# Spatial weights loaded and converted inside the last attention steps of batch 0

## The chip, the cores and the metric

The kernel runs on one core of a Trainium2 chip. The metric is the device time of one execution in microseconds (us). The kernel before took 498.06 us (median of three runs, 496.54 to 500.2).

## The reference

Three blocks follow each other, for a batch of 4 with 576 tokens and 512 channels:

```python
# 1 attention, 8 heads of 64, four with a local and four with a strided mask
scores = where(mask, q @ k.T / 8, -1e9);  x = softmax(scores) @ v
# 2 gated block: h, then a mix over tokens with the spatial weights
h = relu(x @ w_in);  u, v = halves of h
v_n = (v - mean(v)) / sqrt(var(v) + 1e-6)
v_s = einsum('ts,bsd->btd', w_spatial, v_n) + b_spatial
x = (u * v_s) @ w_out
# 3 angles, a mix over tokens, and a residual product
theta = x @ w_theta;  zr, zi = x * cos(theta), x * sin(theta)
y = x + w_tok_r mixed zr + w_tok_i mixed zi;  out = y + relu(y @ w_ch)
```

The weights of w_in, w_out, w_theta, w_tok and w_ch arrive as float64 and are turned into pairs of float16 (high and low part) on the chip. The spatial weights arrive as float32. A matrix product of such pairs is three float16 products (high by high, low by high, high by low).

## The kernel before

Four batches pass one after another. For each, `main_v` makes v (TensorE), relu and mean and variance (ScalarE and VectorE), and `norm`, which normalises v and splits it into `vn`. `main_mid` makes four column blocks of u (`u_chunk`), of the token mix (`sp_chunk`, which reads `vn` and the spatial weights `wsp`, `wspt`), then x2 and theta; `main_end` makes the token mix y and the last product.

Attention of batch 0 has nothing to hide behind. `attention0` runs it in eleven steps (s = 0 to 10) over eight groups of blocks, as a pipeline: in step s TensorE makes the scores of group s (into `pm`), VectorE shifts them, ScalarE takes the exponential; group s-1 is transposed into the bank `av` and copied by ScalarE; group s-2 is multiplied by its values; group s-3 goes into `xT`. `av` is one single bank: whatever writes it in step s waits until ScalarE has copied the group of step s-1 out of it. In steps 1 to 5 a step begins with `WARM` = 6 products of an identity matrix into `av`, whose result nobody reads.

Other work is put into the steps by the dictionary handed to `attention0`: three lists per step, run before, in the middle and at the end of it. It holds the conversions of w_in. Each of eight blocks (`wv[0..3]` for v, `wu[0..3]` for u; `win_piece`) has a load on SP's queue ([0]), two ScalarE instructions ([1], [2]), one VectorE instruction ([3]), and the split into the high part (ScalarE) and the low part (GpSimd) ([4]). `go` advances `main_v(0)` by one part, `step` starts batch 1's attention, which loads its first k, q and v.

While the names in `pinned` are set, that is until `pinned.clear()` after `attention0`, each engine and SP's queue run what is issued in the order of the program. What comes later is ordered by a planner, and may pass the pinned work where an engine would otherwise stand. The later conversions (`conv`) are called by `others()` at due times, counted in TensorE's columns.

The spatial weights: `CONV_SP` gives three due times, which `others()` meets only after `attention0`. `sp_part(0)`, `sp_part(2)` and `sp_tail` each load a block into a staging region, make the high part on ScalarE and the low part on VectorE. The regions are raw0 (`x2f`) and raw1 (the front of `zf`), in which `wv[0]`, `wv[1]` and `wv[2]`, `wv[3]` are staged before. The mask of batch 3 is loaded by `load_mask16`; its tile shares three buffers with those of u.

Of the kernel before, what the change touches and what calls it, by code (L numbers as in the profile page):

```python
# [14 lines left out]
F32 = mybir.dt.float32  # L15
# [3 lines left out]
AF = mybir.ActivationFunctionType  # L19
ALU = mybir.AluOpType  # L20
# [4 lines left out]
SPS = 1024.0  # L25
# [30 lines left out]
WARM = 6  # L56
LEAD = 3.0
ATT_AT = (None, (2.7, 4.2), (86.0, 5.4), (174.5, 4.6))
PREP_AT = (112.0, 126.0, 131.0)
CONV_SP = (20.0, 9.9, 1.9)  # L60
CONV_OUT = (37.0, 12.0, 5.0)
CONV_TH = (49.0, 17.0, 5.0)
TOK_AT = (27.5, 29.5)
# [7 lines left out]
def kernel(  # L71
# [52 lines left out]
    nc = Engines  # L124
# [17 lines left out]
    B, DM, S = out.shape  # L142
    P = 128
    NC = DM // P
    NF = S // P
    T0 = NF * P
    TL = S - T0
# [47 lines left out]
    wsp = const.tile([P, 2, NF, S], F16, name="wsp")  # L195
    wspt = const.tile([P, 2, S], F16, name="wspt")
# [21 lines left out]
    def s2(name):  # L218
        return scr.tile([P, 2, HS * 2], F32, tag="s2", name=name, bufs=4)
# [4 lines left out]
    def pm(name):  # L224
        return ps_m.tile([P, 2, 512], F32, tag="pm", name=name)

    def pa(tag):
        return ps_a.tile([P, 512], F32, tag=tag, name=tag)
# [11 lines left out]
    early = [True, 0]  # L240


    raw0 = x2f.rearrange("p c n -> p (c n)").bitcast(I64)
    raw1 = zf[:, 0:8 * S].bitcast(I64)
# [4 lines left out]
    def stage(late_raw=None):  # L249
        i = early[1]  # L250
        early[1] += 1
        if early[0]:
            return (raw0, raw1)[i % 2], vals[i % 2]
        return late_raw, s2("wx").rearrange("p a n -> p (a n)")
# [21 lines left out]
    def pair(ap, n):  # L276
        return ap[:, 0:2 * n].rearrange("p (a n) -> p a n", a=2)
# [27 lines left out]
        for i in range(0, NC, 2):  # L305
            yield lambda i=i: prep_w(dst, src, slice(0, DM), i, late)

    def sp_part(i):
        stg = pair(stage()[0].bitcast(F32), S)
        nc.sync.dma_start(stg, w_spT[i * P:(i + 2) * P, :].rearrange("(a p) n -> p a n", p=P))  # L310
        nc.scalar.activation(wsp[:, 0, i:i + 2, :], stg, AF.Copy, scale=SPS)
        nc.vector.scalar_tensor_tensor(wsp[:, 1, i:i + 2, :], stg, SPS, wsp[:, 0, i:i + 2, :],
                                       op0=ALU.mult, op1=ALU.subtract)

    def sp_tail():
        stg = pair(stage()[0].bitcast(F32), S)
        for j in range(2):
            nc.sync.dma_start(stg[j * TL:(j + 1) * TL, 0, :], w_spT[T0:S, :])
        nc.scalar.activation(wspt[:, 0, :], stg[:, 0, :], AF.Copy, scale=SPS)
        nc.vector.scalar_tensor_tensor(wspt[0:TL, 1, :], stg[0:TL, 0, :], SPS, wspt[0:TL, 0, :],  # L320
                                       op0=ALU.mult, op1=ALU.subtract)

    def bias_load():
        t = s1("bias")
        for r in (TL, 96):
            nc.gpsimd.dma_start(t[r:r + 1, :], b_sp)
        return t

    def bias_hi(t):
        for r in (TL, 96):  # L330
            nc.scalar.activation(wspt[r:r + 1, 1, :], t[r:r + 1, :], AF.Copy, scale=SPS)
# [130 lines left out]
    def load_q(b, hp, q, c0, c1, by):  # L462
        by.dma_start(q[:, c0:c1], qp[b, hp][:, c0:c1])

    def load_k(b, hp, k, c0, c1, by):

        local = hp < 2
        src = kzl[b, hp] if local else kzs[b, hp - 2]
        c0, c1 = (c0 + STRIDE if c0 else 0, c1 + STRIDE) if local else (c0, c1)
        for j in range(2):  # L470
            h = slice(64 * j, 64 * j + 64)
            by.dma_start(k[h, c0:c1], src[h, j, c0:c1])

    def load_qk(b, hp, q, k, c0, c1, by=None):
        load_q(b, hp, q, c0, c1, by or nc.sync)
        load_k(b, hp, k, c0, c1, by or nc.sync)
# [173 lines left out]
    def attention0(aside):  # L650

        xf = xT[1].rearrange("p e c n -> p (e c n)").bitcast(F32)
        vf = wtok.rearrange("p e i n -> p (e i n)").bitcast(F32)
        qk = kts + [xf[:, i * 2 * S:(i + 1) * 2 * S].rearrange("p (j n) -> p j n", j=2) for i in range(2)]
        q, k = [t[:, 0] for t in qk], [t[:, 1] for t in qk]
        v01 = vf[:, 0:18 * VW].rearrange("p (h n d) -> p h n d", h=2, n=9)
        v23 = vf[:, 18 * VW:30 * VW].rearrange("p (h n d) -> p h n d", h=2, n=6)
        v = [v01[:, i] for i in range(2)] + [v23[:, i] for i in range(2)]  # L660
        for hp in (2, 3):
            load_q(0, hp, q[hp], 0, S, nc.sync)
            load_k(0, hp, k[hp], 0, S, nc.scalar)
        nc.scalar.activation(x2f[:, 0, 0:1], halfpi, AF.Exp)
        bias = bias_load()
        make_masks()
        for n in range(2):
            nc.gpsimd.memset(v23[:, n, 0:6, 0:VW:VW - 1], 1.0)
            nc.gpsimd.memset(v01[:, n, 0:9, 0:VW:VW - 1], 1.0)
        load_vs(0, v23, (2, 3), range(5, 8), nc.gpsimd)  # L670
        load_vs(0, v23, (2, 3), range(5))
        for hp in range(2):
            load_qk(0, hp, q[hp], k[hp], 0, S)
        load_vs(0, v23, (2, 3), range(8, 11))
        load_vl(0, v01, (0, 1))
        for f in aside[-1]:
            f()
        bias_hi(bias)
        un = {}
        for s in range(NG + 3):  # L680
            pre, mid, end = aside.get(s, ((), (), ()))
            if 1 <= s < 6:
                wt = pa("av")
                for _ in range(WARM):
                    nc.tensor.matmul(wt[:, 0:P], identb, identb, start=True, stop=True)
            if s < NG:
                sc = pm("a0")
                t = s2("smx")
                sm, pT = t[:, 0, 0:512], t[:, 1, 0:512].rearrange("p (n k) -> p n k", n=4)
                st = att_p.tile([P, 2, 8], F32, tag="st", name="st", bufs=4)  # L690
                un[s] = sm, pT, st
                qd_scores(quads0[s], q, k, sc)
                qd_shift(quads0[s], sc, sm, st)
            for f in pre:
                f()
            if s >= 3:
                sm, pT, st = un.pop(s - 3)
                local = quads0[s - 3][0]
                qd_out(0, quads0[s - 3], pT, pm("xt")[:, 0, :] if local or s == 5 else pa("sc"))
            if 1 <= s <= NG:  # L700
                sm, pT, st = un[s - 1]
                qd_turn(quads0[s - 1], sm, pa4("av"), pT)
            if s < NG:
                qd_exp(quads0[s], un[s][0])
            if s == 0:
                bias_lo(bias)
            for f in mid:
                f()
            if 2 <= s < NG + 2:
                sm, pT, st = un[s - 2]  # L710
                local = quads0[s - 2][0]
                qd_pv(quads0[s - 2], v, pT, pa("sc").unsqueeze(1) if local else pm("pv"), st, pT)
            for f in end:
                f()
# [277 lines left out]
    def main_v(b):  # L992
# [52 lines left out]
        if b == 0:  # L1045
            ps = []

            def some(pr, cs, ts=(0, 1)):
                for c in cs:
                    for t in ts:  # L1050
                        v_mm(ps[pr][:, t, :], 2 * pr + t, c)

            ps.append(pm("v0"))
            some(0, V0_ORDER[:1])
            yield
            some(0, V0_ORDER[1:2])
            ps.append(pm("v1"))
            some(1, V0_ORDER[:2])
            yield
            some(0, V0_ORDER[2:3])  # L1060
            some(1, V0_ORDER[2:3])
            yield
            for pr in range(2):
                some(pr, V0_ORDER[3:])
                v_relu(pr, ps[pr])
            yield
            norm((0, 1))
        for pr in V_ORDER if b else V_ORDER[2:]:
            ps = pm(f"v{pr}")
# [176 lines left out]
    def timed(parts, due, lead, gap):  # L1246
        parts = list(parts)
        for i, f in enumerate(parts):
            conv.append((due - lead - gap * (len(parts) - 1 - i), f))

    timed([lambda i=i: sp_part(i) for i in range(0, NF, 2)] + [sp_tail], *CONV_SP)
    timed(sq_parts(wout, w_out), *CONV_OUT)
    timed(sq_parts(wth, w_th), *CONV_TH)
    conv.append((conv[-1][0], switch))
# [10 lines left out]
    for at, f in [(at, lambda n=n: tok_load(*toks[n])) for n, at in enumerate(TOK_AT)] + [  # L1265
            (at, lambda: next(atts[N32])) for at in PREP_AT] + [(15.0, load_mask16)]:
        i = next((i for i, c in enumerate(conv) if c[0] > at), len(conv))
# [30 lines left out]
        nc.tensor.matmul(wt[:, 0:P], ident, ident, start=True, stop=True)  # L1298
    wv, wu = ([win_piece(half, i, by) for i in range(NC)] for half, by in ((1, nc.sync), (0, nc.sync)))
    v0 = main_v(0)  # L1300

    def go():
        next(v0)
# [3 lines left out]
        4: ((), (), [w[0] for w in wu]),  # L1307
        5: ((), (), wv[2][1:3]),
        6: ((), wv[2][3:4], wv[2][4:] + wv[3][1:3]),
        7: ((), wv[3][3:4], wv[3][4:] + wv[0][1:3] + [go, step]),  # L1310
        8: ((), wv[0][3:4], wv[0][4:] + wv[1][1:3] + [go]),
        9: (wv[1][3:], (), wu[0][1:3] + [go]),
        10: (wu[0][3:] + wu[1][1:4], (), wu[1][4:] + wu[2][1:3] + [go]),
    })
    for f in wu[2][3:] + wu[3][1:]:
        f()
    pinned.clear()
    run_main(v0)
# [93 lines left out]
```

## Time and profile before

| | |
|---|---|
| time, median of three runs | 498.06 us |
| profiled execution | 498.24 us, its span 496.5 us |
| TensorE (PE) busy | 471.1 us, 95% of the span |
| VectorE (DVE) busy | 306.8 us, 62% |
| ScalarE (ACT) busy | 269.5 us, 54% |
| GpSimd (POOL) busy | 75.8 us, 15% |
| mean granted TensorE clock | 0.990 |

A busy share is a mean over stages that have different limits. The stage of interest is the first 85 us. An instruction in the timeline has a start, a duration, the idle time of its engine before it, and what ended this idle time. Durations of neighbours on ScalarE and VectorE overlap by some tenths of a microsecond, so the distance from start to start is what one costs its engine.

### The profile page before, as it was taken

How to read it: one execution, taken by the hardware profiler on the slowest of the kernel's cores; microseconds unless marked ns; L12 is line 12 of the kernel's file. 1: busy time of each engine (PE TensorE's matmuls, PEld its weight loads, DVE VectorE, ACT ScalarE, POOL GpSimd, SP SyncE). 2: the span in 40 equal slices, each digit the busy share in tenths (PEclk: the TensorE clock that was granted, in tenths of full speed). 3: DMA queues.
4: the chain of work that ended last, by engine and by line, in shares of the span. 5: the costliest groups of instructions: out<-in, count | busy, mean ns of one | idle time of the engine just before them, and what ended most of it. 6: DMA issues, size and time to landing. Idle time of an engine off the chain costs nothing. (4 is left out here: it accounts for less than half of the span.)

```text
span 496.5 us, 10872 instructions
## 1 busy us (share of the span) xinstructions
PE 471.1 (95%) x4476; PEld 353.1 (71%) x4476; DVE 306.8 (62%) x653; ACT 269.5 (54%) x488; POOL 75.8 (15%) x72
## 2 busy tenths in 40 slices
PE   7989687989999999999999999999999999999997
PEld 5754465867577777777658777777657777777775
DVE  4764998877798654863588587872587121217412
ACT  3378677869964344445864766754862022148302
POOL 4014135300004300111002310021005200210220
PEclk9979899999999999999999999999999999999999
DMA  8795647466690045210284156321160020003502
GB/s 205 198 320 177 213 154 239 140 223 176 162 205 1 3 162 164 63 34 1 46 177 127 32 129 175 71 46 20 40 152 2 1 96 1 0 2 68 125 1 96
DMA packets 71421, 52.72 MB, mean 106 GB/s; under 512 B 50713, under 2 KB 59285, under 8 KB 71371
## 3 DMA queue, kind: packets, MB, share of 16 engines
q1 hardware_dynamic: 70843, 51.26, 37.2%
q8 instruction: 35, 0.57, 0.5%
q10 hardware_dynamic: 320, 0.59, 0.5%
q0 software_dynamic: 208, 0.17, 0.1%
q14 instruction: 15, 0.12, 0.1%
HBM read 35.36 MB, written 4.72 MB: 81 GB/s over the span
## 5 line engine op out<-in xcount | busy, mean ns | idle before, releaser
L108 PE MATMUL y<-wtok,zf 128*128 128x288 f16 x864 | 107.2, 286 | 0.0
L108 PEld LDWEIGHTS <-zf 128*128 128x128 f16 x864 | 84.1, 98 | 22.2 <-issue 1.2
L108 PE MATMUL u<-xT,win 128*128 128x288 f16 x384 | 50.9, 291 | 4.6 <-ACT win L108 2.9
L108 PE MATMUL sp<-wsp,vn 128*128 128x288 f16 x384 | 50.2, 286 | 1.3 <-ACT u L108 1.3
L108 PE MATMUL v<-win,xT 128*128 128x512 f16 (+1 forms) x240 | 49.5, 386 | 0.0
L108 PE MATMUL x<-zf,wout 128*128 128x288 f16 x384 | 49.4, 286 | 0.0
L108 PEld LDWEIGHTS <-win 128*128 128x128 f16 x384 | 37.9, 99 | 15.2 <-ACT win L108 3.2
L108 PEld LDWEIGHTS <-vn 128*128 128x128 f16 x416 | 40.5, 98 | 11.3 <-issue 1.4
L108 PE MATMUL th<-x2h,wth 128*128 128x288 f16 x384 | 47.9, 286 | 0.2 <-DVE x2h L108 0.2
L108 PE MATMUL c<-x2h,wch 128*128 128x288 f16 x360 | 45.2, 286 | 0.0
L108 PEld LDWEIGHTS <-wth 128*128 128x128 f16 x384 | 37.6, 98 | 9.8 <-issue 0.4
L108 PEld LDWEIGHTS <-wch 128*128 128x128 f16 x384 | 37.4, 98 | 9.2
L108 PEld LDWEIGHTS <-wout 128*128 128x128 f16 x384 | 36.8, 98 | 9.5
L108 POOL TENSOR_TENSOR x2h<-x2f,x2h 128x576 f16<-128x576 f32 x19 | 27.1, 1429 | 102.8 <-DVE x2h L108 45.1
L108 PEld LDWEIGHTS <-xT 128*128 128x128 f16 (+1 forms) x240 | 21.1, 101 | 25.5 <-issue 2.4
L108 ACT ACTIVATE x2h<-x2f 128x576 f16<-128x576 f32 (+2 forms) x28 | 19.9, 712 | 28.4 <-DVE x2f L108 28.1
L108 ACT ACTIVATE o<-c 128x576 f32<-128x576 f32 x15 | 9.7, 646 | 34.9 <-PE c L108 34.7
L108 DVE TENSOR_TENSOR ta<-ta,x2f 128x1152 f32<-128x1152 f32 (+1 forms) x17 | 21.7, 1283 | 10.9 <-ACT ta L108 10.9
L108 DVE SCALAR_TENSOR_TENSOR x2f<-y,x2f 128x576 f32<-128x576 f32 x16 | 12.0, 753 | 25.1 <-PE y L108 25.1
L108 POOL TENSOR_TENSOR zf<-u,zf 128x576 f16<-128x576 f32 x8 | 10.2, 1281 | 112.6 <-ACT zf L108 112.6
L108 DVE TENSOR_TENSOR u<-u,sp 128x576 f32<-128x576 f32 x16 | 12.0, 750 | 24.1 <-PE sp L108 24.1
L108 DVE SCALAR_TENSOR_TENSOR o<-x2f,o 128x576 f32<-128x576 f32 (+1 forms) x17 | 12.2, 722 | 23.6 <-ACT o L108 23.6
(147 smaller groups left out, 738.4 us busy)
## 6 DMA issues: line engine op xcount, KB each, us to landing
out_dram<-o SPq DMA_DIRECT2D x15, 288.0 KB
kt<-in_qp_dram SPq DMA_DIRECT2D x10, 288.0 KB
qs<-in_qd_dram SPq DMA_DIRECT2D x8, 288.0 KB
zf<-in_w_in_dram SPq DMA_DIRECT2D x4, 512.0 KB
xT<-in_w_ch_dram SPq DMA_DIRECT2D x2, 1024.0 KB
kt<-in_kzl_dram SPq DMA_DIRECT2D x12, 152.0 KB
ks<-in_kl_dram SPq DMA_DIRECT2D x4, 304.0 KB
v<-in_vl_dram SPq DMA_DIRECT2D x8, 144.0 KB
```

What stands on the lines that cost most here:

```text
L108: ins = f(*args, **kwargs)
```

## The change

Without the due times `CONV_SP`, the spatial blocks are handed to `attention0` as steps: the load of the first block in the middle of step 7, its ScalarE half in the middle of step 8, its VectorE half at the end of step 8, with the load of the 64 last rows (the tail) behind it; the load of the second block in step 9 as soon as `wv[1][3]` has read its region; tail and second block are converted in step 10. The conversions of the u blocks each move forward by about half a step, so that `wu[2]` is finished in the middle of step 10 and the ScalarE instructions of `wu[3]` stand between the two last parts of v. `main_v(0)` has one more stop (one `go` for each pair of token blocks of the last channel block), and `early[1] = 1` keeps the alternation of the staging regions. Steps 6 and 7 get `2 * WARM` = 12 idle products each.

```diff
-CONV_SP = (20.0, 9.9, 1.9)
...
-    def sp_part(i):
-        stg = pair(stage()[0].bitcast(F32), S)
...
+    def sp_piece(i, raw):
+        stg = pair(raw.bitcast(F32), S)
+        return [
+            lambda: nc.sync.dma_start(stg, w_spT[i * P:(i + 2) * P, :].rearrange("(a p) n -> p a n", p=P)),
+            lambda: nc.scalar.activation(wsp[:, 0, i:i + 2, :], stg, AF.Copy, scale=SPS),
+            lambda: nc.vector.scalar_tensor_tensor(wsp[:, 1, i:i + 2, :], stg, SPS, wsp[:, 0, i:i + 2, :],
+                                                   op0=ALU.mult, op1=ALU.subtract)]
+
+    def sp_tail(raw):
...
-            if 1 <= s < 6:
+            if 1 <= s < 8:
                 wt = pa("av")
-                for _ in range(WARM):
+                for _ in range(WARM if s < 6 else 2 * WARM):
                     nc.tensor.matmul(wt[:, 0:P], identb, identb, start=True, stop=True)
...
             for pr in range(2):
                 some(pr, V0_ORDER[3:])
                 v_relu(pr, ps[pr])
-            yield
+                yield
             norm((0, 1))
...
-    timed([lambda i=i: sp_part(i) for i in range(0, NF, 2)] + [sp_tail], *CONV_SP)
...
+    sps = [sp_piece(i, raw) for i, raw in ((0, raw1), (2, raw0))] + [sp_tail(raw1)]
+    early[1] = 1
...
-        7: ((), wv[3][3:4], wv[3][4:] + wv[0][1:3] + [go, step]),
-        8: ((), wv[0][3:4], wv[0][4:] + wv[1][1:3] + [go]),
-        9: (wv[1][3:], (), wu[0][1:3] + [go]),
-        10: (wu[0][3:] + wu[1][1:4], (), wu[1][4:] + wu[2][1:3] + [go]),
+        7: ((), wv[3][3:4] + sps[0][:1], wv[3][4:] + wv[0][1:3] + [go, step]),
+        8: ((), wv[0][3:4] + sps[0][1:2], wv[0][4:] + wv[1][1:3] + sps[0][2:] + sps[2][:1] + [go]),
+        9: (wv[1][3:4] + sps[1][:1] + wv[1][4:] + wu[0][1:3], wu[0][3:4], wu[1][1:3] + wu[0][4:] + [go]),
+        10: (wu[1][3:] + wu[2][1:3] + sps[2][1:2], sps[2][2:] + wu[2][3:], sps[1][1:] + [go] + wu[3][1:3] + [go]),
     })
-    for f in wu[2][3:] + wu[3][1:]:
+    for f in wu[3][3:]:
         f()
```

## Rows read from the trace of the kernel before

**Rows 1.** Busy time by stage: us, PE, PEld, DVE, ACT, POOL, granted clock, DMA share, GB/s.

```profile
0.00:25.00 25.00, 21.11 (x337) 16.59 (x341) 15.16 (x40) 9.00 (x17) 6.16 (x21) 1.00 0.78 202
...
29.00:36.00 7.00, 6.31 (x36) 3.89 (x38) 3.10 (x10) 4.88 (x11) 2.33 (x2) 0.51 1.03 354
...
53.00:57.00 4.00, 0.42 (x2) 0.11 (x2) 4.00 (x13) 1.90 (x4) 1.16 (x1) 0.94 0.66 217
57.00:60.00 3.00, 2.98 (x13) 1.92 (x14) 3.00 (x13) 1.90 (x3) 1.02 (x1) 0.51 0.99 365
60.00:69.50 9.50, 8.17 (x98) 6.18 (x97) 9.50 (x25) 8.24 (x12) 3.67 (x4) 1.00 0.43 129
...
110.00:496.50 386.50, 378.99 (x3385) 287.87 (x3382) 223.30 (x457) 197.21 (x365) 44.50 (x31) 1.00 0.30 76
```

**Rows 2.** Timeline, ScalarE, steps 5 to 10 and after: start, us, instruction, idle before.

```profile
25.37 0.58 ACT L108 ACTIVATE smx<-av 96x512 f32<-96x512 f32 x1
...
35.41 0.38 ACT L108 ACTIVATE xT<-xt 128x256 f16<-128x256 f32 x1 [1.70 <-PE xt L108]
...
47.57 2.54 ACT L108 ACTIVATE vr<-v 128x1024 f32<-128x1024 f32 x3
...
50.02 1.15 ACT L108 ACTIVATE wsp<-zf 128x1152 f16<-128x1152 f32 x1
51.07 0.67 ACT L108 ACTIVATE wspt<-x2f 128x576 f16<-128x576 f32 x1
```

**Rows 3.** Timeline, VectorE, from step 6 to the last spatial block.

```profile
26.39 0.55 DVE L108 TENSOR_REDUCE st<-a 128x4 f32<-128x384 f32 x1
...
31.23 0.68 DVE L108 SCALAR_TENSOR_TENSOR x2h<-zf,x2h 128x512 int32<-128x512 int32 x1
...
46.05 1.36 DVE L108 SCALAR_TENSOR_TENSOR wsp<-x2f,wsp 128x1152 f16<-128x1152 f32 x1 [0.32 <-ACT wsp L108]
48.61 0.69 DVE L108 BATCH_NORM_STATS2 bs<-vr 128x6 f32<-128x512 f32 x1 [1.21 <-ACT vr L108]
...
51.74 1.33 DVE L108 SCALAR_TENSOR_TENSOR wsp<-zf,wsp 128x1152 f16<-128x1152 f32 x1
...
53.66 0.73 DVE L108 SCALAR_TENSOR_TENSOR wspt<-x2f,wspt 64x576 f16<-64x576 f32 x1
```

**Rows 4.** Timeline, TensorE, u and the first token mix of batch 0.

```profile
55.78 0.42 PE L108 MATMUL u<-xT,win 128*128 128x288 f16 x2 [2.89 <-ACT win L108]
57.02 4.52 PE L108 MATMUL u<-xT,win 128*128 128x288 f16 x24 [0.82 <-POOL win L108]
...
69.48 1.63 PE L108 MATMUL sp<-wsp,vn 128*128 128x288 f16 x12 [1.33 <-ACT u L108]
```

**Rows 5.** Timeline, TensorE, steps 5 to 8.

```profile
21.95 0.49 PE L108 MATMUL av<-identb 128*128 128x128 bf16 x6
...
24.74 0.56 PE L108 MATMUL a<-kt 64*64 64x96 f32 x16
...
32.20 2.74 PE L108 MATMUL v<-win,xT 128*128 128x512 f16 x6
...
36.47 4.06 PE L108 MATMUL v<-win,xT 128*128 128x512 f16 x18
```

**Rows 6.** Timeline, SP's issues of loads, and one user of a load.

```profile
28.45 0.33 SPq L108 DMA_DIRECT2D kt<-in_qp_dram  x1
...
66.50 0.53 SPq L108 DMA_DIRECT2D zf<-in_w_th_dram  x1
...
73.88 1.17 ACT L108 ACTIVATE zf<-zf 128x1024 f32<-128x1024 f32 x1 [1.01 <-DMA zf<-in_w_th_dram]
```

**Rows 7.** Timeline, GpSimd, low parts of `wu[1]` and `wu[2]`.

```profile
46.61 1.81 POOL L108 TENSOR_TENSOR win<-x2h,win 128x512 f16<-128x512 f32 x1 [1.68 <-ACT win L108]
...
55.80 1.16 POOL L108 TENSOR_TENSOR win<-x2h,win 128x512 f16<-128x512 f32 x1 [7.38 <-ACT win L108]
```

**Rows 8.** VectorE by groups, 44 to 57 us: least, median, most ns; first and last start.

```profile
L108 DVE TENSOR_SCALAR rs<-rs x2: 143/470/796, 55.7 to 56.2; 128x4 int32<-128x4 int32 x2
```

More of the change, by code (lines that the diff above doesn't have):

```diff
@@ L306, in sq_parts, with load @@
             yield lambda i=i: prep_w(dst, src, slice(0, DM), i, late)
-    def sp_part(i):
-        stg = pair(stage()[0].bitcast(F32), S)
[L310 to L321, printed above, removed]
+    def sp_piece(i, raw):
[6 more added lines that the diff above has]
+    def sp_tail(raw):
+        stg = pair(raw.bitcast(F32), S)
+        def load():
+            for j in range(2):
+                nc.sync.dma_start(stg[j * TL:(j + 1) * TL, 0, :], w_spT[T0:S, :])
+        return [
+            load,
+            lambda: nc.scalar.activation(wspt[:, 0, :], stg[:, 0, :], AF.Copy, scale=SPS),
+            lambda: nc.vector.scalar_tensor_tensor(wspt[0:TL, 1, :], stg[0:TL, 0, :], SPS, wspt[0:TL, 0, :],
+                                                   op0=ALU.mult, op1=ALU.subtract)]
     def bias_load():
```

## The prediction

> **What bounds now.** I read the busy time by stage first, then the timeline of each engine from 20 to 85 us. From 110 us on TensorE is busy 379.0 of 386.5 us at clock 1.00 [rows 1]: what the head gains or loses should stay to the end. The head is where the change works, and there TensorE is held up twice: its clock is at 0.51, the lower of its two levels (1.2 GHz of 2.4), from 29 to 36 us and from 57 to 60 us, and from 53 to 57 us it is busy 0.42 of 4 us. The reader should see beside it that VectorE is busy 4.00 of 4, 3.00 of 3 and 9.50 of 9.5 us in the stages from 53 to 69.5 us [rows 1]. From the first statistics of v at 48.61 us, ahead of which it stood 1.21 us for ScalarE's relu of 47.57 us [rows 2, 3], VectorE works off a backlog, at whose end stands the normalised `vn`, and the first token mix, which reads it, starts at 69.48 us [rows 4]. So the question is when VectorE starts on the statistics and how much it has to do from there, not when TensorE has u.
>
> **Idle products.** Six take 0.49 us [rows 5], so twelve take some 0.9. They write `av`, so they also wait for ScalarE's copy out of it, and the scores of the step stand behind them. In step 6 the scores began at 24.74; the copy ended at 25.37 + 0.58 = 25.95 [rows 2, 5]. Now they begin at 25.95 + 0.9 = 26.85, 2.1 us later. VectorE had other work until 26.39 [rows 3] and can shift these scores when they end, near 27.75: 1.4 us later. In step 7, by the same walk, ScalarE and VectorE are 0.7 to 1.2 us late. What they give back: the clock was 1.00 through the steps that have six [rows 1]; if it stays there, six value products cost 1.3 us for 2.74 (eighteen take 4.06, 0.225 each, at the upper level) [rows 5], and the transposes around them some 1.0 us less. TensorE then begins the eighteen products at 35.0 instead of 36.47 us, and ScalarE's first instruction of step 8 starts at 34.7 instead of 35.41 us, before which it stood 1.70 us for TensorE [rows 2, 5]. Term: -0.7 us at the head of step 8, between +0.5 (clock not held) and -1.3.
>
> **First spatial block.** Its load waits for the conversion `wv[3][3]`, which ended at 31.23 + 0.68 = 31.91 us [rows 3] and with the above ends at about 33.0. Batch 1's first loads, issued from 28.45 us [rows 6], stand behind it on SP and slip some 5 us; they are used only after the value products, so I cost that at nothing, and if the cover went, batch 1's first scores would wait. ScalarE reaches the block's high part at about 35.2 us, and if the block isn't there it stands, with `wv[0]`, `wv[1]` and all later conversions behind it. Landing: at least 0.59 MB at the 354 GB/s of that stretch [rows 1], 1.7 us, which costs nothing; at most the 7.4 us of the 1 MB block that was issued at 66.50 behind two other loads and waited for until 73.88 [rows 6]. With nothing ahead of it this block is nearer to the first: I take 3.4 us, landed at 36.4, and ScalarE stands 1.2 us. The Trainium skill ("DMA: Bandwidth & Descriptors", Anatomy of one DMA, stated for loads from GpSimd's queue) gives about 2.0 us plus the bytes at 436 GB/s, an estimate of 3.4 us here; no wait in the trace of before shows this block's landing.
>
> **ScalarE until the relu.** Ahead of the first relu now also stand the second block's high part (50.02 to 51.07, 1.05 from start to start), the tail's (some 0.57) [rows 2] and the high part of `wu[2]` (some 0.5): +2.1 us; the first block's was there before. The two instructions of `wu[3]` (1.1) come before the second relu only. In the pinned order of steps 8 to 10 ScalarE also waits for VectorE, for 0.6 us conversions and the tail's 0.73 us; it did so before, with less VectorE work in between, so I add 0.8. Sum: -0.7 + 1.2 + 2.1 + 0.8 = +3.4; some of it falls where ScalarE stood in before, so I take +2.8: relu at about 50.4, statistics from 51.4 instead of 48.61 us.
>
> **VectorE from there.** It no longer has to do, after that moment, the second block's low part (1.33), the tail's (0.73) and the conversion of `wu[2]` (0.68 by its like), 2.5 us from start to start [rows 3]. Nor does it meet GpSimd's low part of `wu[2]` (55.80 to 56.96 us [rows 7]), beside which a small instruction of the variance took 796 instead of 143 ns [rows 8]: -0.65. Statistics 2.8 later, work 3.2 less: `vn` comes 0.4 us earlier. Against it, the same kind of meeting is new in steps 8 and 9, where the low part of `wsp` (1.36) and GpSimd's low part of `wv[0]` fall together. The row at 46.61 shows such a pair: GpSimd took 1.81 for 1.16 us beside the `wsp` of 46.05 [rows 3, 7]. Between nothing and 1.2 us on VectorE's next conversion I take 0.5. Sum for `vn`: +0.1 us, bounds -1.9 (block landed in time, no meeting) to +3.
>
> The Trainium skill ("SBUF — State Buffer", SBUF: two separate sides) has a rule that speaks against the change here: of a GpSimd instruction and a VectorE one with two inputs in SBUF, the later stands until the other is done. By that rule the conversion of `wv[1]` would stand for all of GpSimd's 1.16 us, and the sum would be 0.7 us longer; rows 8 agree with it for one small instruction, and no row shows it for a conversion.
>
> **TensorE's waits.** The 2.89 and 0.82 us in which u waits for its weights can go, and some 1.5 us of clock (24 products in 4.52 us [rows 4]; by columns, at the rate of the eighteen, 3.0). But the token mix doesn't wait for u: what TensorE saves before 69.48 us it will spend waiting for `vn`, or for the buffers that the later relu sets free, so I count nothing. One thing can move: at 69.48 us it had waited 1.33 us for the relu of the third u block [rows 4], held up by the mask of batch 3, whose load follows TensorE's progress. I take half, -0.65, of 0 to -1.3.
>
> **Sum.** The profiled execution is 498.24 us, span 496.5 and 1.7 around it, 0.2 above the median. 498.24 + 0.1 - 0.65 = 497.7; against the median 497.5. I forecast no change.
>
> **Rivals.** *TensorE is what counts.* If VectorE only looks full, its planner having filled time with work that could wait, and `vn` follows u, the 2.89, 0.82, 1.5 and 1.33 us of TensorE's waits are all won: 498.1 - 6.5 = 491.6 us. For it: TensorE is idle or slow there. Against: VectorE has no idle time from 53 to 69.5 us [rows 1]. Chance 0.12.
>
> *ScalarE stands for the first spatial block.* This wait takes the place of the one removed, in step 8, with the whole pinned order behind it. Each microsecond after 36.4 moves the relu, the statistics and `vn` by one; landing 7.4 us after its issue, like the block of 66.50, gives +4.0: 501.5 us. It decides from 37.5 us on, and is over 1% slower from 41.5. For it: the load is some 2 us old when ScalarE comes to it, and the DMA share is 1.03 in that stretch [rows 1]. Against: w_in's blocks should be through by then, and batch 1's loads queue behind. Chance 0.13.
>
> *The clock falls nevertheless*, and the idle products only hold up the scores: +0.5 instead of -0.7 in step 8, 498.7 us. For it: TensorE mostly waits in steps 6 to 8. Chance 0.07.
>
> **Numbers.** The forecast has 0.68. Its own range is 495.5 to 500, since the bounds -1.9 and +3 hardly come together with those of the other term. To leave no more than 2 in 10 outside I leave out the first rival and the upper half of the second: 494.5 to 501. Within 1% (about 5 us, what can be told from no change here) lie the forecast, the third rival and most of the second: 0.82. Faster by over 1%: 0.11, nearly all the first rival; slower: 0.07, the worst of the second.
>
> **What will show it.** Clock 1.00 from 29 to 36 us, and the eighteen products at about 35 us. A wait of ScalarE for the spatial block in step 8. The first relu of v between 49.5 and 51.5 us, and the statistics right behind it. u without a wait for its weights, but a wait of TensorE for `vn`, buffers or VectorE in its place, and the first token mix at 68.5 to 70 us. I am wrong if the first token mix comes before 66 us, or if the relu is not later than in before.

## The result and the profile after: 0.75% slower

The changed kernel takes 501.91 us (median of 20 runs), the kernel before 498.7 (20 runs beside them): ratio 1.0075 [1.0051, 1.0099], by which it is some 3.75 us slower (the medians lie 3.2 us apart). I had forecast no change (497.5) in a range that ended at 501. The profiled spans are 500.6 and 496.5 us.

The busy time by stage of the changed kernel, columns as in [rows 1]:

```profile
29.00:36.00 7.00, 6.45 (x70) 3.74 (x68) 4.72 (x16) 5.05 (x11) 2.32 (x2) 1.00 0.91 337
53.00:57.00 4.00, 3.66 (x29) 2.54 (x30) 4.00 (x11) 3.25 (x6) 0.00 (x0) 0.50 0.65 255
57.00:60.00 3.00, 3.00 (x19) 2.09 (x18) 3.00 (x14) 2.36 (x3) 1.38 (x1) 0.71 0.00 0
60.00:69.50 9.50, 8.23 (x94) 6.15 (x91) 8.58 (x25) 5.85 (x9) 3.60 (x3) 1.00 0.66 218
66.00:72.00 6.00, 2.23 (x28) 1.42 (x25) 6.00 (x7) 2.98 (x4) 5.87 (x5) 1.00 1.01 345
72.00:79.00 7.00, 6.56 (x41) 4.43 (x42) 6.78 (x13) 5.40 (x9) 1.24 (x2) 0.53 0.01 2
110.00:500.60 390.60, 383.46 (x3435) 291.22 (x3434) 225.85 (x466) 200.37 (x375) 43.43 (x31) 1.00 0.30 77
```

The clock is 1.00 from 29 to 36 us, where [rows 1] had 0.51. From 53 us TensorE has work at once, but at the lower level. The new hole is from 66 to 72 us: TensorE busy 2.23 of 6 us while VectorE is full, and right behind it the clock is 0.53 for seven microseconds. From 110 us on nothing is new: 7.1 us of idle time, 7.5 in [rows 1].

ScalarE, VectorE, GpSimd, TensorE and SP in the same kernel, from their timelines (start, us, instruction, idle before):

```profile
24.73 0.58 ACT L107 ACTIVATE smx<-av 96x512 f32<-96x512 f32 x1
...
36.12 1.16 ACT L107 ACTIVATE wsp<-zf 128x1152 f16<-128x1152 f32 x1 [1.61 <-DMA zf<-in_w_spT_dram]
...
50.25 1.00 ACT L107 ACTIVATE vr<-v 128x1024 f32<-128x1024 f32 x1
```

```profile
38.97 1.27 DVE L107 SCALAR_TENSOR_TENSOR x2h<-x2f,x2h 128x512 int32<-128x512 int32 x1 [0.30 <-ACT x2h L107]
...
51.66 0.68 DVE L107 BATCH_NORM_STATS2 bs<-vr 128x6 f32<-128x512 f32 x1
...
61.00 1.21 DVE L107 SCALAR_TENSOR_TENSOR x2h<-x2f,x2h 128x1024 int32<-128x1024 int32 x1
...
63.15 1.23 DVE L107 SCALAR_TENSOR_TENSOR x2h<-zf,x2h 128x1024 int32<-128x1024 int32 x1 [0.80 <-ACT x2h L107]
...
66.14 5.26 DVE L107 TENSOR_SCALAR vr<-vr,mv,rs 128x512 f32<-128x512 f32 x4
...
72.48 2.34 DVE L107 TENSOR_TENSOR vn<-vr,vn 128x1024 f16<-128x1024 f32 x2
```

```profile
37.88 1.81 POOL L107 TENSOR_TENSOR win<-x2h,win 128x512 f16<-128x512 f32 x1 [3.79 <-ACT win L107]
...
65.90 5.22 POOL L107 TENSOR_TENSOR wout<-x2h,wout 128x512 f16<-128x512 f32 x4 [6.10 <-ACT wout L107]
```

```profile
31.29 1.47 PE L107 MATMUL v<-win,xT 128*128 128x512 f16 x6
34.25 4.06 PE L107 MATMUL v<-win,xT 128*128 128x512 f16 x18
...
54.49 6.54 PE L107 MATMUL u<-xT,win 128*128 128x288 f16 x35
...
72.37 1.12 PE L107 MATMUL sc<-pT,v 96*64 96x64 f32 x16 [4.04 <-DVE rs L107]
...
74.50 5.40 PE L107 MATMUL sp<-wsp,vn 128*128 128x288 f16 x24
```

```profile
32.26 0.39 SPq L107 DMA_DIRECT2D zf<-in_w_spT_dram  x1
...
48.09 0.39 SPq L107 DMA_DIRECT2D zf<-in_w_out_dram  x1
51.76 0.38 SPq L107 DMA_DIRECT2D x2f<-in_w_out_dram  x1
```

Against them five rows of the kernel before that the prediction had not asked for, on VectorE, GpSimd and SP:

```profile
61.91 1.23 DVE L108 SCALAR_TENSOR_TENSOR x2h<-zf,x2h 128x1024 int32<-128x1024 int32 x1
63.05 1.91 DVE L108 TENSOR_SCALAR vr<-vr,mv,rs 128x512 f32<-128x512 f32 x4
...
66.28 3.55 DVE L108 TENSOR_TENSOR vn<-vr,vn 128x1024 f16<-128x1024 f32 x2
```

```profile
64.91 2.28 POOL L108 TENSOR_TENSOR wout<-x2h,wout 128x512 f16<-128x512 f32 x2 [4.77 <-ACT wout L108]
```

```profile
53.10 0.37 SPq L108 DMA_DIRECT2D zf<-in_w_out_dram  x1
```

The reader should see four things. Ahead of the normalise now stand **both** conversions of w_out, with a wait between them (1.21 + 0.80 + 1.23); before, one did. The normalise itself, four `TENSOR_SCALAR`, takes 5.26 us instead of 1.91, beside four low parts of w_out on GpSimd; before, two started when it was nearly over. Part of that price had been paid elsewhere: in the kernel before, GpSimd's work stood beside the low part of `vn`, which took 3.55 us; now that is 2.34 (72.48), 1.2 us less. And the load of w_out's first block is issued 5.0 us sooner than before.

The head of the program runs up to 3 us sooner or later from one profiled execution to the next, so I count from ScalarE's copy of step 5 (25.37 us before, [rows 2]; 24.73 after). Microseconds behind that copy, with the kernels of the next section; "theta" is the first product with w_theta, "v, batch 1" the first of its 60 products in a row, and from there to the end all take 368 to 370 us:

| kernel | relu | normalise | token mix | theta | v, batch 1 | end |
|---|---|---|---|---|---|---|
| before | 22.20 | 37.68 | 44.11 | 89.92 | 102.01 | 471.13 |
| after | 25.52 | 41.41 | 49.77 | 95.13 | 107.37 | 475.87 |
| e1, GpSimd's parts late | 25.93 | 41.98 | 46.55 | 93.76 | 106.02 | 474.67 |
| e2, conversions late | 25.76 | 37.53 | 42.35 | 89.74 | 103.01 | 470.99 |
| e4, before + idle products | 20.67 | 34.95 | 41.21 | 86.82 | 98.58 | 467.09 |
| f2, e4 + u sooner | 21.76 | 35.73 | 41.16 | 86.82 | 98.58 | 466.87 |
| f4, e2 + second block late | 24.50 | 37.14 | 42.65 | 88.75 | 100.51 | 468.57 |
| g1, before + conversions late | 20.79 | 35.16 | 43.33 | 90.26 | 102.02 | 472.21 |
| g2, f2 + conversions late | 21.75 | 34.20 | 40.60 | 87.48 | 103.10 | 471.69 |

After is 5.7 us behind before at the token mix and 5.4 at v of batch 1: the loss arises ahead of the token mix and stays. In the spans 0.64 us of it is hidden by the earlier head. Each row is a single execution, and e2's (499.51 us) is the slowest of its 12 runs (median 497.19): the timed runs, not the last column, say what a change is worth.

### The profile page after: what moved, and what is told of

The parts are those of the page before. It is cut to its first block, busy times and chain, and to the rows that moved or that the text cites. A ratio compares the mean times of both kernels' runs of the same rounds, so it can differ in the third digit from the quotient of the medians.

```text
span 500.6 us, 10919 instructions
## 1 busy us (share of the span) xinstructions
PE 473.7 (95%) x4500; PEld 354.7 (71%) x4500; DVE 308.0 (62%) x653; ACT 269.8 (54%) x488; POOL 74.3 (15%) x72
## 5 line engine op out<-in xcount | busy, mean ns | idle before, releaser
L107 PE MATMUL sp<-wsp,vn 128*128 128x288 f16 x384 | 52.6, 294 | 0.1
```

The costliest lines, as they stand in the source:

```text
L107: ins = f(*args, **kwargs)
```

## The experiments

Two causes were set against each other: **A**, w_out's conversions ahead of the normalise and GpSimd's parts beside it; **B**, the relu that comes 3 us later. Ratios are to the kernel before, in four sets of runs, each on one chip.

**First set.** e1 lets GpSimd's low parts of w_out (and of w_theta) wait for vn's; e2 puts only the VectorE conversions of w_out behind it, as an order and not as a wait.

```diff
# e1, on the changed kernel (in both, normed[0] is the instruction of vn's low part)
-            N[E_WLO[late]].tensor_tensor(dst_lo[:, a], x[:, a], dst_hi[:, a], ALU.subtract)
+            low = N[E_WLO[late]].tensor_tensor(dst_lo[:, a], x[:, a], dst_hi[:, a], ALU.subtract)
+            if late == 1:
+                behind_vn(low, mybir.DependencyClass.Sync)
# e2, on the changed kernel, in prep_w
+            if f is fs[2] and dst is wout:
+                behind_vn(ins, mybir.DependencyClass.NoSync)
```

> The kernel after, but GpSimd's low parts of w_out (and of w_theta) wait for the low part of vn. Theory A (the loss is the meeting of GpSimd's four w_out instructions with VectorE's normalise, which took 5.3 us for 1.9): the four normalising instructions take about 2 us, the first token mix starts near 71 us instead of 74.5, and the time falls by 2.5 to 4 us, to a ratio of 0.999 to 1.003 to the kernel before. Theory B (the loss is the first relu of v, 2.7 us later on ScalarE, whatever w_out does): at most 1 us comes back, ratio 1.005 or more.

Measured: e1 1.0067 [1.0041, 1.0092], nothing gained. By its own line (1.005 or more) e1 falls on B's side; its trace, below, says why A is not out.

> The kernel after, but VectorE's conversions of w_out are queued behind vn's low part on VectorE (and their GpSimd parts follow). Theory A: the meeting is gone and two conversions of 1.2 us and a wait of 0.8 us no longer stand ahead of the normalise; it starts near 63 us and takes 2, the token mix starts near 68 to 69 us, ratio 0.994 to 1.000. Theory B: statistics still begin near 51.7 us, so vn gains no more than the 1.2 us of one conversion, ratio 1.004 or more.

Measured: e2 1.0001 [0.9977, 1.0025]. VectorE and TensorE of e1, then VectorE and TensorE of e2:

```profile
67.11 1.91 DVE L107 TENSOR_SCALAR vr<-vr,mv,rs 128x512 f32<-128x512 f32 x4
...
75.04 1.59 DVE L107 TENSOR_TENSOR vn<-vr,vn 64x512 f16<-64x512 f32 x1
```

```profile
71.68 3.10 PE L107 MATMUL sp<-wsp,vn 128*128 128x288 f16 x24 [0.43 <-ACT u L107]
...
76.69 0.42 PE L107 MATMUL sp<-wspt,vn 128*128 128x288 f16 x2 [1.67 <-DVE vn L107]
78.25 0.42 PE L107 MATMUL sp<-wspt,k 128*128 128x288 f16 x2 [1.14 <-POOL k L107]
```

```profile
64.24 1.92 DVE L107 TENSOR_SCALAR vr<-vr,mv,rs 128x512 f32<-128x512 f32 x4
...
72.39 1.22 DVE L107 SCALAR_TENSOR_TENSOR x2h<-zf,x2h 128x1024 int32<-128x1024 int32 x1
```

```profile
69.06 1.87 PE L107 MATMUL sp<-wsp,vn 128*128 128x288 f16 x13
...
126.78 3.10 PE L107 MATMUL th<-x2h,wth 128*128 128x288 f16 x24 [1.34 <-DVE ta L107]
```

In e1 the meeting is gone from the normalise (1.91 again) and the token mix starts 3.2 us sooner, but the four parts then fall on the tail of vn and ahead of the copy of `k`, and TensorE waits 1.67 and 1.14 us there. Both conversions still stand ahead of the normalise, which comes as late as in the changed kernel (41.98 in the table, 41.41). In e2 the relu is as late as in the changed kernel, and yet the normalise comes 3.9 us sooner and the token mix 7.4: for the start of the token mix A is shown, as a whole: e2 moves the two conversions and the meeting together, and no run prices them one by one. Of that 7.4 us the end of the profiled execution keeps 4.9, and the runs 0.74%, some 3.7 us (0.66% against e1, which stands in the same set); some is spent on a wait at theta.

**Idle products**, taken out of the changed kernel (e3) and put alone into the one before (e4, the diff reversed):

```diff
-            if 1 <= s < 8:
+            if 1 <= s < 6:
...
-                for _ in range(WARM if s < 6 else 2 * WARM):
+                for _ in range(WARM):
```

> The kernel after without idle products in steps 6 and 7. If they give what was predicted (0.7 us at the head of step 8): clock near 0.5 from 29 to 36 us, relu of v about 0.7 us later than 50.25, ratio about 1.009. Rival (they only hold up the scores, or ScalarE and VectorE set the pace there anyway): relu at 49.5 to 50.3 us, ratio 1.005 to 1.0075. If they are a part of the loss of 3.75 us, ratio below 1.004.

> The kernel before with the twelve idle products in steps 6 and 7 and nothing else. If the predicted term holds: clock 1.00 from 29 to 36 us, step 8 0.7 to 2 us sooner, ratio 0.996 to 0.999. Rival (what they gain is lost to VectorE's backlog): clock 1.00, step 8 sooner, statistics of v no sooner than 48.4 us, ratio 0.999 to 1.001.

Measured: e3 1.0142 [1.0106, 1.0178], e4 0.9941 [0.9913, 0.9969]. The idle products are worth 0.7% in the one and 0.6% in the other, some 3 us; the rest of the change costs what e3 shows, 7 us. So the loss of 3.75 us is 7 us lost and 3 won, and e2, level with the kernel before, is still 0.6% behind e4. e4 by stage, and its token mix:

```profile
29.00:36.00 7.00, 6.42 (x75) 3.98 (x73) 4.73 (x15) 5.48 (x13) 2.33 (x2) 1.00 0.90 299
53.00:57.00 4.00, 3.42 (x26) 2.12 (x24) 4.00 (x20) 2.60 (x6) 1.16 (x1) 1.00 0.18 59
57.00:60.00 3.00, 2.11 (x25) 1.54 (x26) 3.00 (x12) 1.74 (x3) 1.15 (x1) 1.00 0.44 94
```

```profile
66.42 1.75 PE L108 MATMUL sp<-wsp,vn 128*128 128x288 f16 x13 [1.62 <-ACT u L108]
```

The clock now holds not only from 29 to 36 us but also from 53 to 60, and the planner puts both conversions of w_out behind the token mix's start (at 68.94 and 70.72 us). The profiled execution of e3, one of several, happens to have this:

```profile
29.00:36.00 7.00, 5.66 (x69) 3.44 (x65) 4.79 (x14) 5.75 (x13) 2.33 (x2) 1.00 0.86 317
```

Clock 1.00 without the idle products: one profile doesn't price them, the timed runs do. Over these the mean granted clock is 0.980 in e3 against 0.986 in the changed kernel, and 0.987 before against 0.993 in e4.

**Second set**, on the parts. f1 is e4 with e2's rule, f2 is the kernel before with idle products and u's conversions sooner (the spatial blocks left to the planner), f4 is e2 with the second spatial block behind the relus, f6 is e4 with batch 3's mask load due later.

```diff
# f2, on the kernel before (also: the idle products, and wu's pieces half a step sooner in steps 9 and 10)
-            yield
+                yield
             norm((0, 1))
# f4, on e2
-        10: (..., sps[1][1:] + [go] + wu[3][1:3] + [go]),
+        10: (..., [go] + wu[3][1:3] + [go] + sps[1][1:]),
# f6, on e4
-            ... + [(15.0, load_mask16)]:
+            ... + [(50.0, load_mask16)]:
```

> The kernel before with the idle products, and with VectorE's conversions of w_out queued behind vn's low part. Theory A (w_out ahead of the normalise costs wherever it stands there): before has one such conversion, 1.2 us, ahead of it; vn comes 1 to 1.5 us sooner, ratio 0.990 to 0.994. Rival (only the two together that the change brought forward cost): ratio 0.993 to 0.997, as with the idle products alone.

> The kernel before with the idle products and u's conversions half a step sooner, the spatial blocks left to the planner at their due times. If the spatial blocks in pinned order are what costs (ScalarE's late relu, w_out's early staging): ratio 0.991 to 0.996. If the sooner conversions of u cost as well, because they stand ahead of the relu of v on ScalarE: ratio 0.997 to 1.003.

> The kernel after with w_out's conversions behind vn's low part and the second spatial block converted behind the two relus of v instead of ahead of them. Theory B (the late relu is what is left of the loss once w_out is out of the way): the relu comes 1.1 to 1.6 us sooner, and with it vn and the token mix, ratio 0.996 to 0.9985 against 1.0001. Rival (the order within VectorE's backlog doesn't matter, only its length): 0.9985 to 1.0015.

> The kernel before with the idle products, and batch 3's mask loaded at due time 50 instead of 15. If the wait of TensorE ahead of the first token mix (1.3 us in before) is the mask's, as the prediction had it: the wait is gone, ratio 0.991 to 0.993. If vn's low part comes no sooner, it only changes its name: 0.993 to 0.996.

Measured: f1 0.9926 [0.9898, 0.9953], f2 0.9922 [0.9897, 0.9948], f4 0.9965 [0.9941, 0.9988], f6 0.9913 [0.9893, 0.9933]. f1 has the order of e4 on TensorE, VectorE, ScalarE, GpSimd and SP, since the planner had put both conversions behind by itself; so it measures e4 again, within 0.15% across the two sets, and doesn't test A. u's conversions sooner cost nothing (f2); so what costs 1.5%, from f2 to the changed kernel, is the placing of the spatial blocks, with the order that the planner makes around it. With w_out and the second block out of the way (f4) 0.4% of it is left, beside 1.5 us at the token mix against f1 (42.65 and 41.17). f6 has the lowest ratio, but the 0.13% to f1 are inside the noise: its token mix still waits 0.77 us for ScalarE's relu of u, 1.62 in e4, and the mask's part of that wait is gone.

**Third set**, e2's rule elsewhere: g1 on the kernel before, g2 on f2, g4 on f2 with f6's mask; g3 is f4 with the first block and the tail behind the relus too.

```diff
# g3, on f4: first block and tail out of steps 8 and 10, behind the relus
-        8: ((), wv[0][3:4] + sps[0][1:2], wv[0][4:] + wv[1][1:3] + sps[0][2:] + sps[2][:1] + [go]),
+        8: ((), wv[0][3:4], wv[0][4:] + wv[1][1:3] + [go]),
...
+        10: (..., [go] + wu[3][1:3] + [go] + sps[0][1:] + sps[2][:1] + sps[1][1:] + sps[2][1:]),
```

> The kernel before, no idle products added, with w_out's conversions on VectorE behind vn's low part. In the run with idle products alone the planner had put them there by itself, and it gained 0.6%. Theory A (a conversion of w_out ahead of the normalise costs its length): 1.0 to 1.6 us of that gain are this order, ratio 0.9965 to 0.9985, and the normalise starts near 62 instead of 63 us. Rival (the idle products and the clock made all of the gain): ratio 0.999 to 1.001.

> The kernel before with idle products and u's conversions sooner, with w_out's conversions behind vn's low part. Without the latter it was at 0.9922 with one conversion ahead of the normalise, which took 3.6 us for 1.9. Theory A: 2 to 3 us less, ratio 0.986 to 0.989. Rival (GpSimd's work then meets something else as late): 0.990 to 0.993.

> The kernel after with w_out's conversions behind vn's low part, and all three spatial blocks loaded in the same steps or later, but converted behind the two relus of v. With only the second block there it was 0.9965. If ScalarE's wait for the first block (1.6 us) and the standing of wv[1]'s conversion behind GpSimd (0.6 us) are the rest of the loss: relu 2 to 3 us sooner, ratio 0.989 to 0.993. If the rest is VectorE's backlog, which gets the blocks back: 0.995 to 0.998.

> The kernel before with idle products, u's conversions sooner, w_out's conversions behind vn's low part, and batch 3's mask at due time 50. If the mask's wait is still the last one ahead of the token mix: another 1 us off g2. Rival: the same as g2 within 0.5 us.

Measured: g1 0.9992 [0.9962, 1.0021], g2 0.9999 [0.997, 1.0028], g3 1.0009 [0.9987, 1.0031], g4 0.9966 [0.9935, 0.9998]. The first three are slower than theory A has them; g4 lies 0.33% under g2, as it was to, but that is inside the noise. In g1 the normalise comes 2.5 us sooner than in the kernel before (1.4 of it with the relu) and the runs gain nothing. That bears on two things: A is not shown to cost time where one conversion stands ahead of the normalise, only where two do, with four of GpSimd's parts; and since g1 has w_out's conversions behind, as e4, without the idle products, this order makes little or nothing of what e4 gains. g2 is ahead of f2 at the token mix (40.60 and 41.16) and gives back more than it won: w_th's second block is loaded later (issued at 89.03 us, 71.44 in f2), which puts theta 0.7 us behind f2, and then comes a wait. ScalarE and TensorE of g2:

```profile
120.16 0.73 ACT L108 ACTIVATE xT<-xT 128x576 f32<-128x576 f32 x1 [3.23 <-DMA xT<-in_w_ti_dram]
```

```profile
123.00 4.77 PE L108 MATMUL th<-x2h,wth 128*128 128x288 f16 x24 [2.03 <-DVE ta L108]
```

ScalarE stands 3.23 us for the last load of w_ti, the angles' work stands behind it, TensorE waits 2.03 us and does the 24 products partly at the lower clock (4.77 us for 3.10; 0.66 granted from 123 to 128 us). That is 3.7 of the 3.9 us that g2 loses between theta and v of batch 1. Why that load is late is not the rule's doing alone: f1 has e4's order, issues the load at the same time, and yet:

```profile
113.35 0.34 SPq L108 DMA_DIRECT2D xT<-in_w_ti_dram  x1
```

```profile
117.07 0.74 ACT L108 ACTIVATE xT<-xT 128x576 f32<-128x576 f32 x1 [0.16 <-DMA xT<-in_w_ti_dram]
```

```profile
113.31 0.34 SPq L108 DMA_DIRECT2D xT<-in_w_ti_dram  x1
```

```profile
119.95 0.73 ACT L108 ACTIVATE xT<-xT 128x576 f32<-128x576 f32 x1 [3.07 <-DMA xT<-in_w_ti_dram]
```

(The first two are e4, the others f1.) Up to the start of its user the load takes 6.6 us instead of 3.7 with nothing else changed, and f1's span is 1.7 us longer than e4's. In g2, g3 and g4 it takes 5.6 to 6.6 us, in g1 at most 4.0. How much of the third set's loss is this spread, and how much the later loads, stays open. g3 shows another price: its relu (20.86 us behind the copy) and normalise (34.81) are as early as e4's, but the tail is loaded at 53.53 us, ScalarE stands 3.92 us for it ahead of u's next weights, and the token mix starts at 43.27.

**Fourth set.** h4 is the changed kernel with w_out due later, h2 is f4 with f6's mask, h1 is f2 with f6's mask.

```diff
# h4, on the changed kernel
-CONV_OUT = (37.0, 12.0, 5.0)
+CONV_OUT = (37.0, 3.0, 3.0)
```

> The changed kernel with one constant of w_out's due times moved, so that its planner puts the second of w_out's two VectorE conversions (1.2 us, and the 0.8 us that VectorE stood for it) behind the normalise of v, and the first stays ahead of it. Theory A (the loss is w_out's conversions ahead of the normalise and GpSimd's low parts beside it): half the dose is gone, so the normalise starts some 2 us sooner (at most 39.5 us behind the copy of step 5, against 41.4 in the changed kernel), two of GpSimd's four low parts still meet it, it takes 3 to 4 us instead of 5.3, and the time lies about half way between the changed kernel (1.0075 of before) and the one with both conversions behind vn (1.0001): 1.003 to 1.005. Theory B (the loss is the later relu, whatever stands behind it): relu unchanged, so 1.007 or more.

> The changed kernel with w_out's conversions behind vn, the second spatial block behind the relus and batch 3's mask load due later: what is left of the change's cost against the kernel before with idle products and the same late mask (0.9913 of before) is the first block's, the tail's and u's conversions ahead of the relu. Theory A: nothing much is left, the mask's wait of 0.8 us at the token mix goes too: 0.992 to 0.996. Theory B: the relu still 2.3 to 3.8 us late costs at least 2 us more than in that kernel: 0.996 or more. If the last load of the tokens' weights lands 6 us after its issue instead of 4, as in some profiles, 2 us come on top between 120 and 127 us.

> The kernel before with idle products in steps 6 and 7, u's conversions half a step sooner and batch 3's mask load due later; the spatial blocks stay with the planner. This is the version that the experiments point to. Theory A: u's conversions sooner are worth nothing by themselves, because one of w_out's conversions comes ahead of the normalise and meets GpSimd, so 0.990 to 0.992, as without them (0.9913). If sooner conversions of u help after all: under 0.990.

Measured: h4 1.0058 [1.0029, 1.0087], h2 0.9992 [0.9958, 1.0026], h1 0.9958 [0.993, 0.9985]. h4's constant moved more than it was meant to: a load of w_tr is issued at 49.86 us, ahead of w_out's, and it no longer computes what the reference does, so it doesn't separate the theories. h1 should have been at f6's 0.991 and f2's 0.992; if it is no worse than they are, sets of runs differ by some 0.4%, and smaller differences between sets are read no further. (f2 against g2, and the changed kernel against e2, are such differences, of 0.8 and 0.7%.) h2 falls on B's side (0.996 or more). Within this set h2 is 0.34% behind h1, as f4 was 0.4% behind f1: some 1.8 us remain for the blocks ahead of the relu, and that is my estimate of what B is worth. Each of the two differences is only about as large as its noise, and g3, whose relu is early again, did not win them back, so B is not shown.

## Why the prediction was wrong, by its own steps

*Idle products* was right in its mechanism, and at the head of step 8 in its size; what comes of it later was too small. The clock held and the eighteen products came at 34.25 us (forecast 35.0). ScalarE's first instruction of step 8 (its copy into `xT`) starts at 33.86 us, 9.13 behind the copy of step 5, for 10.04 before: -0.9 us, where I took -0.7. But I followed it only to there. e4 has the relu 1.5 us earlier, the normalise 2.7, the token mix 2.9, and the runs gain 0.59%, 2.9 us: what I called worthless for u, the clock from 53 to 60 us, came with it. How the 2.9 us divide between the two, no run separates.

*First spatial block* was right: ScalarE stood 1.61 us (1.2), 3.86 us after the issue (3.4 landed). The Trainium skill ("DMA: Bandwidth & Descriptors", Anatomy of one DMA) gave an estimate of 3.4 us, for loads from GpSimd's queue; the trace has 0.46 more on SP's, up to the start of the instruction that waited. The rival of the late block is out: the kernel became slower, but not by that wait.

*ScalarE until the relu* was right: relu at 50.25 us (50.4), statistics at 51.66 (51.4). That it comes so near is in part luck: behind the copy the relu is 3.3 us later than before, not 2.8, and the head happened to run 0.64 us sooner. 3.3 is near the sum of 3.4 from which I took 0.6 off.

*VectorE from there* is the step that failed. That VectorE has 3.2 us less to do, and so makes good the later relu, holds for the greater part: with w_out's conversions behind vn in both, it is 11.77 us from the relu to the normalise in e2 and 14.37 in g1, 2.6 us less. That e2's normalise comes when it did in the kernel before (37.53 and 37.68) needs one thing more: the one conversion that stood ahead of it there is gone, too. From the relu to the normalise the changed kernel takes 15.89 us and the kernel before 15.48. I counted what left VectorE's queue and took the rest of the queue as given. But its planner filled the place with w_out's other conversion, and thereby brought four of GpSimd's low parts onto the normalise. I had looked for new meetings in steps 8 and 9, found one there, rightly priced (0.59 us on the conversion at 38.97, 0.5 forecast), and not asked where the meetings of the moved work would be. Price: the normalise 3.7 us later and 3.35 us longer, of which the low part of `vn` gives back 1.2: 5.9 in sum, close to the 5.7 us by which the token mix is late. Then comes the clock (24 products in 5.40 us for 3.10). The bound of +3 didn't hold a second full meeting.

Whether the planner moved them because w_out's loads are issued sooner, or because its VectorE had room, no run separates.

*TensorE's waits*: u no longer waits for its weights, as forecast, and the wait of 4.04 us for VectorE stands in their place. Counting their gain at nothing was right (f2, with u's weights sooner, gains no more than f1); that the new wait would bring the lower clock was missed. The mask's wait is gone too, for nothing, as everything came later.

The rival "TensorE is what counts" is out for the changed kernel, and "The clock falls nevertheless" for the stretch that it spoke of (1.00 from 29 to 36 us). Of the signs, the token mix at 74.50 us (68.5 to 70 forecast) is the one that failed.

## What to carry to other kernels

When work is taken out of a queue that a planner fills, the freed time isn't free: look in the order for what moves into it, and what that meets on another engine. Restore the order of the displaced work before judging the move; here that gave back 0.74%, as much as was lost, though the kernel stayed 0.6% behind the one with the idle products alone. And follow a gain or a loss two stages on: 7.4 us at the token mix were 4.9 at the end of the profiled execution and 3.7 in the timed runs.

## What the runs showed of the hardware

The groups of the changed kernel from 66 to 72 us (busy us, mean ns | idle before):

```profile
L107 DVE TENSOR_SCALAR vr<-vr,mv,rs 128x512 f32<-128x512 f32 x4 | 5.3, 1374 | 0.0
L107 POOL TENSOR_TENSOR wout<-x2h,wout 128x512 f16<-128x512 f32 x4 | 5.2, 1334 | 6.1 <-ACT wout L107 6.1
```

The same `TENSOR_SCALAR` takes 541 ns in the kernel before. Here four of one engine and four of the other went in turn: each VectorE one starts some 0.24 us behind a GpSimd one, ends 0.28 us behind it, and is as long. Alone, from start to start, one takes 0.46 us on VectorE and 1.12 on GpSimd in the kernel before; a pair takes 1.30 here and not the sum of 1.58, so some 0.3 us of each pair still overlap.

The Trainium skill ("SBUF — State Buffer", SBUF: two separate sides) gives the shared ports to whoever starts first, for its whole instruction, and counts VectorE's faster two-port mode beside two inputs in SBUF. The trace agrees, but for these 0.3 us, if these instructions run in that mode, which no run here shows by itself. I had applied the rule to two inputs alone; and the instruction of [rows 8], with which I called the rows in agreement, reads one tensor, so they didn't bear on the rule as I had put it.
